# Strassen's scheme in the last FFN stage of two token tiles, and DMA transposes for the local heads of the last batch

## The chip, the cores and the metric

The kernel runs on one core of one Trainium2 chip. The metric is the device time of one execution in microseconds. Four executions of the kernel before took 269.8, 269.98, 270.36 and 271.9 us, with a median of 270.17 us.

## What is computed

The reference is sparse attention followed by a multiplicative feed-forward network (FFN):

```python
batch, n_heads, seq, head_dim = (8, 8, 576, 64)
mask_local = (rel >= 0) & (rel < 32)                                  # heads 0 to 3
mask_strided = (rel >= 0) & (pos[None, :] % 32 == pos[:, None] % 32)  # heads 4 to 7
attn = softmax(where(mask, scale * q @ k.T, -1e9)) @ v
x = attn.transpose(0, 2, 1, 3).reshape(4608, 512)
out = ((x @ w1) * (x @ w2)) @ w3 @ w_out        # w1, w2: 512 x 1024, w3: 1024 x 1024, w_out: 1024 x 512
```

Inputs and output are float32. The kernel multiplies in float16 and adds up in float32.

## The kernel before

**Planner.** The kernel is a list of operations (`plan.op`) with an engine, an assumed duration, dependencies, buffer slots taken and given back, and a rank. `Plan.order` plays this list through once with its own assumed durations and so fixes one order for each engine; the operations are then emitted in that order. Semaphores come from the dependencies of the tiles, in program order. SP issues all DMAs, in one queue.

**Stages.** The product w34 = w3 @ w_out is formed first. Attention goes batch by batch, and within a batch by pairs of heads: pairs 0 and 1 are local, 2 and 3 strided. For each pair there are scores on TensorE (`ps_S`, L795), the Exp on ACT (L812), the mask on DVE (L819) and the product with v (`ps_X`, L831 or L843). A strided pair is normalised by Ln and Exp on ACT and a product on DVE, straight into `xT` (L904). A local pair is normalised on DVE into `xqs` (L866, L867) with the token on the partition; six TensorE transposes (`ps_U`, L924) and one DVE copy then bring it into `xT`. A second way exists in the code: from batch `UB` on, the local pair is normalised into `xqd` and a DMA transpose on SP (L914) writes `xT`. `UB` is 8 before, so it is not used. `xT[0]` to `xT[3]` hold the attention output, feature on the partition and token on the free axis, one tile for each pair of heads.

**FFN.** There are nine tiles of 512 tokens. For tiles 0 to 6, each of eight columns jc of 128 features has four matmuls with w1 (`ps_a`, L1119), four with w2 (`ps_b`, L1135), an ACT copy of a, and a DVE product into `abt` (L1141). Then each of four blocks of 128 tokens has eight matmuls of 128x512 with w34 (`ps_o`, L1155), an ACT copy into `osb` (L310) and a store.

**The last two tiles**, tA = 7 and tB = 8, use Strassen's scheme (in Winograd's form) for the columns named in `sf`, which before are 1 to 7. The two tiles and the two halves of the 512 input features make a 2x2 block matrix, w1 and w2 with the same halves the other one. Seven products P1 to P7 of two matmuls each (L1053) replace eight. The sums of inputs are called S1 to S4 (L990, on POOL and DVE), the differences of weights T1 to T4 (L965, POOL). The products are gathered in a bank A (`ps_Aw`) and in a tile of two banks, E and G (`ps_Bw`), in this order: P1 into A, P5 into G, A copied onto E by ACT (`e`), P6 into A, G copied out by ACT (`p5`), P2 into E, A copied out (`u2`), P7 into A, G plus u2 on DVE (`u4`, L1076), E copied out (`c11`), A plus p5 on DVE (`c22`, L1084), P3 into G, P4 into A, and at last the two products into `abt` (L1088, L1091). Column 0 is done in the plain way for both tiles, and all eight output blocks of the two tiles are plain. The last block is split by columns into 256, 128 and 128.

Of the kernel before, what the change touches and what calls it, by code (L numbers as in the profile page):

```python
# [24 lines left out]
def _loads():  # L25
# [6 lines left out]
    for b in range(2, 8):  # L32
# [6 lines left out]

CFG = dict(loads=_loads(), arank=_arank, frank=lambda j: 50 + j, slack=100,  # L40
           pord=lambda b: (2, 3, 0, 1) if b < 2 else (0, 1, 2, 3), tsplit=False, dmaf=1.08, nhr=8, cast=dict(w1=dict(POOL=1040)),
           first=('DVE', 'ACT', 'POOL'), early=0, pm=4, nx=4, nstg=8, new=(2, 3), lb=3, ll=4, nat={'POOL': 1160}, sf=(1, 2, 3, 4, 5, 6, 7), te={'POOL': 2150}, nr=(1, 25, 2, 0), te1='POOL', se=((3, 0), (3, 1), (1, 0), (2, 0), (4, 0)))


def _ap(t: bass.AP, off_add, dims):
# [215 lines left out]
def kernel(  # L261
# [38 lines left out]
    NABT = cfg.get("nabt", 3)  # L300
    stgs = [consts.tile([P, DF], FP32, name=f"st{i}") for i in range(NSTG)]
    plan = Plan(dict(f=NF, B=2, stg=NSTG, asb=2, osb=3, rcp=2, xqs=2, xqd=cfg.get("nxq", 2), w3n=3, abt=NABT,
                     u2=2, p5=2, c11=2, c22=2))

    def pin(ins):
        return tc.keep_in_program_order(ins)
# [259 lines left out]
    def load_qs(b, hp):  # L566
        hh, local = hp % 2, hp < 2
        b1 = LL if local else LB
        for nm, ten in (("q", q), ("k", k)):
            key = f"{nm}s{b}_{hp}"  # L570
            if local:
                ds = [dma(key, key, 880, [P, 2, LT, D], lambda s: s[0:LQ].rearrange("p h c d -> p h (c d)"),
                          ten[b, 2 * hp:2 * hp + 2].rearrange("h (p c) d -> p h (c d)", c=LT))]
            else:
                ds = load_s(key, ten, b, hp)
            nr, nt = (LQ, LT) if local else (SC, ST)

            def fn(e, nm=nm, key=key, nr=nr, nt=nt):
                t = qkp.tile([nr, nt, 2, D], FP16, tag=f"{nm}{hp // 2}", name="xs16")
                copy(e, t.rearrange("p c h d -> p h c d"), stg[key][0:nr])  # L580
                x16[(b, nm, hp)] = t

            c = cast("c" + key, key, ds, {"POOL": 825} if local else POOL, fn)
            late.append((c, lambda nm=nm: [DTop[(b - 1, nm, hp)]] if b > b1 else
                         [Top.get((b - 2 + hh, h)) for h in (hp - hh, hp - hh + 1)]))

            def ft(e, nm=nm, key=key, nr=nr, nt=nt):
                if local:
                    o = live[key] = ffn.tile([P, nt * nr], FP16, tag="w3n", bufs=3, name="qk8")
                elif nm == "q":  # L590
                    o = qT[:, hp]
                else:
                    o = kTS[:, hh, 0:ST * SC]
                pin(nc.sync.dma_start(o.rearrange("x (c w) -> x c w", w=nr),
                                      x16[(b, nm, hp)].rearrange("p c h d -> p (c h d)"), transpose=True))
# [352 lines left out]
    smul, sfirst = {}, []  # L948
    if SF:
        W = {(1, 1): w1h[:, 0:2], (1, 2): w2h[:, 0:2], (2, 1): w1h[:, 2:4], (2, 2): w2h[:, 2:4]}  # L950
        T, Tt = {}, {}
# [47 lines left out]
        if cfg.get("te1", "POOL") == "POOL":  # L999
            gate = plan.op("gate", {"POOL": 200}, lambda e: pin(  # L1000
                nc.gpsimd.tensor_copy(out=scr, in_=St[1][:, 1, 1, 0:2])), deps=[Sx[(4, 1)], T[(4, 0)]], rank=11)
            for i in range(1, 5):
                T[(i, 1)].deps.append(gate)
        SL = lambda j: (lambda c: St[j // 3][:, (j - 1) % 2 if j < 3 else j - 3, c])
        A = {1: lambda c: xT[c][:, tk1], 2: lambda c: xT[2 + c][:, tk1], 4: lambda c: xT[2 + c][:, tk2]}
        sd = lambda i: [Sx[(i, 0)], Sx[(i, 1)]]
# [8 lines left out]
    for n_, jc in enumerate(SF):  # L1015
# [75 lines left out]
            nc.vector.tensor_mul(big[("abt", tB)][:, jc, :], bk("A"), tmp["c22"])), [q4], give=[kA, tk["c22"]])  # L1091
        smul[(tA, jc)], smul[(tB, jc)] = h1, h2

    def frk(t, jc):
        if not SF or t < tA:
            return 100 + 24 * t + 2 * jc + 1
        i = [x for x in range(KF) if x not in SF].index(jc)
        return 100 + 24 * tA + cfg.get("nr", (1, 25, 2, 0))[t - tA] + cfg.get("nr", (1, 25, 2, 0))[2] * i

    for t in range(NTILE):  # L1100
# [9 lines left out]
        for jc in range(KF):  # L1110
            js = bass.ds(jc * P, P)
            if (t, jc) in smul:
                muls.append(smul[(t, jc)])
                continue

            def fa(e, jc=jc, t=t, js=js, tok=tok):
                ps = bank("f", f"a{t}_{jc}", [P, NT], FP32)
                for ci in range(KM):
                    pin(nc.tensor.matmul(ps, w1h[:, ci, js], xT[ci][:, tok], start=(ci == 0), stop=(ci == KM - 1)))  # L1119

            a = plan.op(f"a{t}_{jc}", {"PE": 864}, fa, deps=[z] + w1c[jc] + (xd if t in zs else []), take=[("f", f"a{t}_{jc}")],
                        rank=frk(t, jc))

            def fs(e, jc=jc, t=t):
                asb = ffn.tile([P, NT], FP32, tag="asb", bufs=2, name="asb")
                live[("asb", t, jc)] = asb
                copy(e, asb, bank("f", f"a{t}_{jc}"))

            s = plan.op(f"asb{t}_{jc}", cfg.get("asb", {"ACT": 590}), fs, deps=[a], take=[("asb", f"{t}_{jc}")],
                        give=[("f", f"a{t}_{jc}")], rank=4)  # L1130

            def fb(e, jc=jc, t=t, js=js, tok=tok):
                ps = bank("f", f"b{t}_{jc}", [P, NT], FP32)
                for ci in range(KM):
                    pin(nc.tensor.matmul(ps, w2h[:, ci, js], xT[ci][:, tok], start=(ci == 0), stop=(ci == KM - 1)))  # L1135
# [7 lines left out]
            muls.append(plan.op(f"mul{t}_{jc}", {"DVE": 690}, fu, deps=[bb, s],  # L1143
                                give=[("f", f"b{t}_{jc}"), ("asb", f"{t}_{jc}")], rank=4))
        for ts in range(NT // P):
# [76 lines left out]
```

## Time and profile before

| | value |
|---|---|
| median of the four runs | 270.17 us |
| profiled execution | 270.19 us, of which the span of the trace is 268.2 us |
| granted TensorE clock, mean | 0.998 |
| first `ps_U` of batch 7, second `ps_U` | 205.12 us, 210.68 us |
| last `ps_X` of batch 7 | 219.98 us |
| first plain column of tile 7 | 224.57 us |
| first P5 | 228.02 us |
| last output matmuls issued from | 252.86 us on, without a break |
| first copy of the last block | 263.94 us |

The page gives the busy time of each engine in the span. Matmuls are pipelined: a row of the timeline that says 0.43 us may have its successor start after 0.27 us, and the distance of the starts is what the path pays. Windows give the same busy times stretch by stretch. The chain of waits goes back from the last instruction to what released each one.

### The profile page before, as it was taken

The page shows a single profiled execution, that of the slowest core. Times are in us where ns is not written, and L with a number is a line of the kernel's source. Part 1 is how long each engine was busy: PE and PEld are TensorE (multiplying, and loading weights), DVE is VectorE, ACT ScalarE, POOL GpSimd, SP SyncE. Part 2 cuts the span into 40 slices and gives each one's busy share as a digit, 9 for nine tenths or more (in the row PEclk, how much of TensorE's full clock was granted, in tenths as well). Part 3 has the DMA queues.
Part 4 walks back from the last instruction along what each step waited for, and adds up shares of the span by engine and source line. Part 5 has one row for each costly group of instructions (what it writes and reads, how often), then busy time and mean ns, then how long its engine had stood idle before and what let it go on. Part 6 is the DMA issues. An engine that isn't in the chain of part 4 may idle for free.

```text
span 268.2 us, 6079 instructions
## 1 busy us (share of the span) xinstructions
PE 256.2 (96%) x2251; PEld 140.0 (52%) x2251; DVE 179.1 (67%) x342; ACT 162.3 (61%) x293; POOL 169.2 (63%) x186
## 2 busy tenths in 40 slices
PE   6787799999999999999999999999999999999994
PEld 2466687545655555554554454455445554434443
DVE  6744566885787748866875788479748865678601
ACT  2780467774666785577477557764785576577241
POOL 6676897769979716955795479617999553900000
PEclk9999999999999999999999999999999999999999
DMA  7999999999799988899999998999994004000053
GB/s 248 316 367 287 302 355 353 323 247 283 282 287 212 175 214 224 192 175 288 225 180 183 280 251 171 194 281 205 179 211 149 2 0 156 0 2 0 0 197 121
DMA packets 72766, 54.41 MB, mean 203 GB/s; under 512 B 44256, under 2 KB 62048, under 8 KB 72736
## 3 DMA queue, kind: packets, MB, share of 16 engines
q1 hardware_dynamic: 72736, 54.02, 82.7%
q8 instruction: 18, 0.29, 0.5%
q14 instruction: 12, 0.10, 0.1%
HBM read 38.93 MB, written 9.44 MB: 180 GB/s over the span
## 4 chain that ended last, share of the span: by engine, by line
PE 86%; DMA 8%; POOL 1%; DVE 1%; ACT 1%; SPq 1%; issue 1%; POOLq 0%; DVEq 0%
PE ps_o L1155 23%; PE ps_b L1135 19%; PE ps_a L1119 18%; DMA st<-in_moe_w_dram 6%; PE ps_Aw L1053 4%; PE ps_S L795 4%; PE ps_Bw L1053 3%; PE ps_mm L670 3%; PE ps_X L843 3%; PE ps_X L831 3%; PE ps_U L924 2%; DMA st<-in_q_dram 2%; PE ps_T L748 2%; SPq L317 1%; POOL w3n L314 1%
## 5 line engine op out<-in xcount | busy, mean ns | idle before, releaser
L1155 PE MATMUL ps_o<-w,abt 128*128 128x512 f16 (+2 forms) x304 | 67.9, 368 | 0.0
L1135 PE MATMUL ps_b<-xT,w2h 128*128 128x512 f16 x232 | 59.4, 379 | 0.2 <-DVE kTL L312 0.2
L1119 PE MATMUL ps_a<-xT,w1h 128*128 128x512 f16 x232 | 59.6, 379 | 0.0
L310 ACT COPY asb<-ps_a 128x512 f32<-128x512 f32 x58 | 34.0, 589 | 31.0 <-PE ps_a L1119 29.9
L1141 DVE TENSOR_TENSOR abt<-ps_b,asb 128x512 f16<-128x512 f32 x58 | 39.9, 688 | 7.6 <-PE ps_b L1135 6.4
L314 POOL CAST xs<-st 80x1024 f16<-80x1024 f32 (+1 forms) x36 | 33.3, 941 | 17.0 <-DMA st<-in_k_dram 10.1
L812 ACT ACTIVATE ps_S<-ps_S 128x576 f32<-128x576 f32 (+2 forms) x56 | 32.9, 627 | 16.3 <-PE ps_S L795 16.3
L1155 PEld LDWEIGHTS <-abt 128*128 128x128 f16 x304 | 27.6, 98 | 28.2 <-issue 0.2
L904 DVE TENSOR_TENSOR xT<-ps_X,rcp 64x288 f16<-64x288 f32 x56 | 25.2, 450 | 18.3 <-ACT rcp L888 17.8
L1135 PEld LDWEIGHTS <-w2h 128*128 128x128 f16 x232 | 21.6, 98 | 23.7 <-issue 0.7
L310 ACT COPY osb<-ps_o 128x512 f32<-128x512 f32 (+1 forms) x36 | 20.3, 581 | 17.8 <-PE ps_o L1155 17.6
L314 POOL CAST v16L<-st 32x768 f16<-32x768 f32 (+1 forms) x32 | 26.3, 823 | 7.0 <-DMA st<-in_v_dram 5.5
L1119 PEld LDWEIGHTS <-w1h 128*128 128x128 f16 x232 | 20.2, 99 | 18.5
L819 DVE TENSOR_TENSOR ptm<-ps_S,maskL 128x576 f16<-128x576 f32 x28 | 19.9, 753 | 9.1 <-ACT ps_S L812 8.9
L867 DVE TENSOR_TENSOR xqs<-ps_X,rcq 96x384 f16<-96x384 f32 (+1 forms) x36 | 20.5, 568 | 1.2
L314 POOL CAST v16S<-st 72x1024 f16<-72x1024 f32 (+1 forms) x16 | 16.5, 1037 | 7.2 <-DMA st<-in_v_dram 7.2
L877 ACT ACTIVATE ps_X<-ps_X 64x576 f32<-64x576 f32 x28 | 17.7, 631 | 3.8 <-PE ps_X L831 3.2
L888 ACT ACTIVATE rcp<-ps_X 64x576 f32<-64x576 f32 x28 | 18.2, 648 | 0.9
L843 PEld LDWEIGHTS <-ptm 128*96 128x96 f16 (+1 forms) x224 | 14.6, 123 | 5.8 <-issue 0.2
L670 PE MATMUL ps_mm<-woh,xT 128*128 128x256 f16 x128 | 16.0, 273 | 1.4 <-POOL woh L314 1.4
L314 POOL CAST x<-st 128x1024 f16<-128x1024 f32 x14 | 14.4, 1038 | 3.6 <-DMA st<-in_q_dram 1.7
L819 DVE TENSOR_TENSOR ptm<-ps_S,maskK 72x576 f16<-72x576 f32 x20 | 14.1, 746 | 2.5 <-ACT ps_S L812 2.5
(113 smaller groups left out, 358.4 us busy)
## 6 DMA issues: line engine op xcount, KB each, us to landing
out_dram<-osb SPq DMA_DIRECT2D x35, 256.0 KB
st<-in_moe_w_dram SPq DMA_DIRECT2D x16, 512.0 KB
st<-in_v_dram SPq DMA_DIRECT2D x16, 288.0 KB
st<-in_v_dram SPq DMA_DIRECT2D x16, 256.0 KB
st<-in_q_dram SPq DMA_DIRECT2D x7, 512.0 KB
st<-in_k_dram SPq DMA_DIRECT2D x7, 512.0 KB
st<-in_q_dram SPq DMA_DIRECT2D x10, 256.0 KB
st<-in_k_dram SPq DMA_DIRECT2D x10, 256.0 KB
```

The source lines that it names most:

```text
L310: pin(nc.scalar.copy(out=out, in_=in_))
L314: pin(nc.gpsimd.tensor_copy(out=out, in_=in_))
L670: pin(nc.tensor.matmul(ps, w3T(kc)[:, js], big["woh"][:, kc, ns], start=(kc == 0), stop=(kc == KF - 1)))
L812: pin(nc.scalar.activation(out=sps, in_=sps, func=AF.Exp, bias=0.0, scale=scale))
L819: pin(nc.vector.tensor_mul(ptm[0:kr, 0:576].rearrange("p (h a x) -> p h a x", h=2, x=w), pte[0:kr].rearrange("p h (a x) -> p h a x", x=w), ...
L843: pin(nc.tensor.matmul(xps[0:w, h, i * 65:(i + 1) * 65], ptms[pslot][0:kr, c0:c0 + w], vt[0:kr, 2 * (hp % 2) + h, g * m + i, 0:D + 1], sta ...
L867: pin(nc.vector.tensor_mul(xqs[0:w, 0:m].rearrange("p i h d -> p h i d"), xv[:, :, :, 0:D], _ap(rcp, 0, [[rcp.ap[0][0], w], [4, 2], [1, m] ...
L904: pin(nc.vector.tensor_mul(o, i0, i1))
L1119: pin(nc.tensor.matmul(ps, w1h[:, ci, js], xT[ci][:, tok], start=(ci == 0), stop=(ci == KM - 1)))
L1135: pin(nc.tensor.matmul(ps, w2h[:, ci, js], xT[ci][:, tok], start=(ci == 0), stop=(ci == KM - 1)))
L1141: pin(nc.vector.tensor_mul(big[("abt", t)][:, jc, :], bank("f", f"b{t}_{jc}"), live[("asb", t, jc)]))
L1155: pin(nc.tensor.matmul(ps, big[("abt", t)][:, ci, bass.ds(ts * P, P)], w34[:, ci, bass.ds(n0, nw)], start=(ci == 0), stop=(ci == KF - 1)))
```

## The change

Four things are changed.

- **Output by Strassen.** For the token blocks 0 and 1 (`so=(0, 1)`) of both last tiles, the product with w34 is done by the same scheme. The blocks are: a token block of tile 7 over one of tile 8, the halves of the 1024 features of `abt` (jc 0 to 3, jc 4 to 7), and w34 cut in two by features and in two by its 512 output columns. One product is four matmuls of 128x256. The differences of w34 go to POOL (`O1` to `O4`), the sums of `abt` to DVE except the third, which goes to POOL (`Z`). The results are put together in float32 in parts of `xT` that are no longer read (`o7`, `o8`) and stored from there. Blocks 2 and 3 stay plain.
- **Which columns are plain.** `sf` is now 0 to 6, so column 7 is plain in the two last tiles.
- **Local heads of batch 7** (`ub=7`) go through `xqd` and two DMA transposes; `nxq=3` gives `xqd` three buffers.
- A key of `x16` is renamed, with no effect.

The planner orders everything anew with this list; the order of the instructions before tile 6 is the same as before.

```diff
-           ... sf=(1, 2, 3, 4, 5, 6, 7), te={'POOL': 2150}, ...)
+           ... sf=(0, 1, 2, 3, 4, 5, 6), te={'POOL': 2150}, ..., so=(0, 1), ro=42, ub=7, nxq=3)
...
+    def out_strassen():
+        HN = DM // 2
+        hh = {(1, 1): (tA, 0), (1, 2): (tA, 4), (2, 1): (tB, 0), (2, 2): (tB, 4)}
+        W = {(i, j): w34[:, 4 * i - 4:4 * i, bass.ds(HN * (j - 1), HN)] for i in (1, 2) for j in (1, 2)}
...
+            T[i] = plan.op(f"O{i}", {"POOL": 2150}, ftt, deps=w34op + [T1last, T.get(1), T.get(2)],
+                           take=[("stg", f"O{i}")] if i in (1, 2) else [], rank=14, lock=True)
...
+        for n_, ts in enumerate(SO):
+            Sx = {}
+            for i in (3, 1, 2, 4):
...
+                d = {3: md(tA, 1) + md(tB, 1), 1: md(tB, 1) + md(tB, 2), 2: md(tA, 1), 4: md(tA, 2)}[i]
+                Sx[i] = plan.op(f"Z{i}_{ts}", {"POOL": 1150} if i == 3 else {"DVE": 430}, fss,
+                                deps=d + ([Sx[i // 2]] if i in (2, 4) else []), rank=3.9 + .01 * n_, lock=True)
+            kA, kB = ("f", f"Ao{ts}"), ("B", f"Bo{ts}")
+            prods = dict(P1=(lambda ts=ts: ah(1, 1, ts), lambda: W[(1, 1)], "A", md(tA, 1) + w34op),
+                         P5=(lambda ts=ts: sv(1, ts), lambda: Tt[1], "G", [Sx[1], T[1]]),
+                         P6=(lambda ts=ts: sv(2, ts), lambda: Tt[2], "A", [Sx[2], T[2]]),
+                         P2=(lambda ts=ts: ah(1, 2, ts), lambda: W[(2, 1)], "E", md(tA, 2)),
+                         P7=(lambda ts=ts: sv(3, ts), lambda: Tt[3], "A", [Sx[3], T[3]]),
+                         P4=(lambda ts=ts: ah(2, 2, ts), lambda: Tt[4], "A", md(tB, 2) + [T[4]]),
+                         P3=(lambda ts=ts: sv(4, ts), lambda: W[(2, 2)], "G", [Sx[4]]))
...
+                    for c in range(4):
+                        pin(nc.tensor.matmul(bk(x), lf()[:, c], rt()[:, c], start=st_ and c == 0, stop=c == 3,
+                                             skip_group_check=not st_))
...
+            ce_ = vec("e", AC, lambda e, bk=bk: copy(e, bk("E"), bk("A")), [q1, q5])
+            q6 = prod("P6", extra=[ce_], rank=.5)
+            c5 = vec("p5", AC, lambda e, bk=bk, new=new: copy(e, new("p5"), bk("G")), [q5], take=["p5"])
+            q2 = prod("P2", extra=[ce_], rank=.6)
+            cu = vec("u2", AC, lambda e, bk=bk, new=new: copy(e, new("u2"), bk("A")), [q6], take=["u2"])
+            q7 = prod("P7", extra=[cu], rank=1)
+            g = vec("u4", DV, lambda e, bk=bk, tmp=tmp: pin(nc.vector.tensor_add(bk("G"), bk("G"), tmp["u2"])),
+                    [cu, c5], give=[tk["u2"]])
+            c22 = vec("c22", DV, ..., [q7, c5], take=["o8"], give=[tk["p5"]])
+            c11 = vec("c11", AD, lambda e, bk=bk, new=new: copy(e, new("o7")[:, 0:HN], bk("E")), [q2], take=["o7"])
+            q3 = prod("P3", extra=[g], rank=1.1)
+            q4 = prod("P4", extra=[c22], rank=1.2)
+            c12 = vec("c12", AD, lambda e, bk=bk, tmp=tmp: copy(e, tmp["o7"][:, HN:DM], bk("G")), [q3, c11], give=[kB])
+            c21 = vec("c21", AD, lambda e, bk=bk, tmp=tmp: copy(e, tmp["o8"][:, 0:HN], bk("A")), [q4, c22], give=[kA])
...
         for ts in range(NT // P):
+            if t in zs and ts in SO:
+                continue
```

In the new order, the TensorE stream from the end of tile 6 is: P1 of columns 0, 1 and 2, P5 of 0 and 1, P6 and P2 of 0, the plain a of tile 7 column 7, and so on through the seven columns; the plain output halves of tile 7 (blocks 2 and 3) stand among the last Strassen products of the FFN. The output products then come in this order (the last digit is the token block): P1-0, P4 of column 6, second halves of blocks 2 and 3 of tile 7, P5-0, P1-1, first half of block 2 of tile 8, P6-0, P2-0, P5-1, P7-0, P3-0, P6-1, P4-0, P2-1, P7-1, P3-1, second half of block 2, P4-1, and the split block 3. On SP, the two DMA transposes stand after the last stores of tile 5 and ahead of those of tile 6.

More of the change, by code (lines that the diff above doesn't have):

```diff
@@ L41 @@
            pord=lambda b: (2, 3, 0, 1) if b < 2 else (0, 1, 2, 3), tsplit=False, dmaf=1.08, nhr=8, cast=dict(w1=dict(POOL=1040)),
-           first=('DVE', 'ACT', 'POOL'), early=0, pm=4, nx=4, nstg=8, new=(2, 3), lb=3, ll=4, nat={'POOL': 1160}, sf=(1, 2, 3, 4, 5, 6, 7), te={'POOL': 2150}, nr=(1, 25, 2, 0), te1='POOL', se=((3, 0), (3, 1), (1, 0), (2, 0), (4, 0)))
+           first=('DVE', 'ACT', 'POOL'), early=0, pm=4, nx=4, nstg=8, new=(2, 3), lb=3, ll=4, nat={'POOL': 1160}, sf=(0, 1, 2, 3, 4, 5, 6), te={'POOL': 2150}, nr=(1, 25, 2, 0), te1='POOL', se=((3, 0), (3, 1), (1, 0), (2, 0), (4, 0)), so=(0, 1), ro=42, ub=7, nxq=3)
 def _ap(t: bass.AP, off_add, dims):
@@ L302 @@
     plan = Plan(dict(f=NF, B=2, stg=NSTG, asb=2, osb=3, rcp=2, xqs=2, xqd=cfg.get("nxq", 2), w3n=3, abt=NABT,
-                     u2=2, p5=2, c11=2, c22=2))
+                     u2=2, p5=2, c11=2, c22=2, ob=4))
     def pin(ins):
@@ L580, in fn @@
                 copy(e, t.rearrange("p c h d -> p h c d"), stg[key][0:nr])
-                x16[(b, nm, hp)] = t
+                x16[(b, nm, "s", hp)] = t
             c = cast("c" + key, key, ds, {"POOL": 825} if local else POOL, fn)
@@ L594, in ft @@
                 pin(nc.sync.dma_start(o.rearrange("x (c w) -> x c w", w=nr),
-                                      x16[(b, nm, hp)].rearrange("p c h d -> p (c h d)"), transpose=True))
+                                      x16[(b, nm, "s", hp)].rearrange("p c h d -> p (c h d)"), transpose=True))
             o = DTop[(b, nm, hp)] = plan.op(f"D{nm}{b}_{hp}", {"SP": 1300}, ft, deps=[c], dma=cfg.get("dtc", (1080, 1200))[0 if local else 1], store=True,
@@ L947 @@
     tk1, tk2 = bass.ds(tA * NT, NT), bass.ds(tB * NT, NT)
-    smul, sfirst = {}, []
+    smul, sfirst, mul = {}, [], {}
     if SF:
@@ L1003 @@
                 T[(i, 1)].deps.append(gate)
+        T1last = T[(4, 1)]
         SL = lambda j: (lambda c: St[j // 3][:, (j - 1) % 2 if j < 3 else j - 3, c])
@@ L1092, with ftt, ah, sv @@
         smul[(tA, jc)], smul[(tB, jc)] = h1, h2
+    SO = cfg.get("so", ()) if SF else ()
+    def out_strassen():
+        HN = DM // 2
+        hh = {(1, 1): (tA, 0), (1, 2): (tA, 4), (2, 1): (tB, 0), (2, 2): (tB, 4)}
+        W = {(i, j): w34[:, 4 * i - 4:4 * i, bass.ds(HN * (j - 1), HN)] for i in (1, 2) for j in (1, 2)}
+        T, Tt = {}, {}
+        for i, x, y in ((1, (1, 2), (1, 1)), (3, (2, 2), (1, 2)), (2, (2, 2), 1), (4, (2, 1), 2)):
+            def ftt(e, i=i, x=x, y=y):
+                if i in (1, 2):
+                    raw = stgs[plan.slot[("stg", f"O{i}")]].bitcast(FP16).rearrange("p (i k n) -> p i k n", i=2, k=4)
+                    Tt[i], Tt[{1: 3, 2: 4}[i]] = raw[:, 0], raw[:, 1]
+                b0 = Tt[y] if isinstance(y, int) else W[y]
+                eng = nc.gpsimd if e == "POOL" else nc.vector
+                pin(eng.tensor_sub(Tt[i], W[x], b0))
+            T[i] = plan.op(f"O{i}", {"POOL": 2150}, ftt, deps=w34op + [T1last, T.get(1), T.get(2)],
+                           take=[("stg", f"O{i}")] if i in (1, 2) else [], rank=14, lock=True)
+        def ah(i, j, ts):
+            t, c0 = hh[(i, j)]
+            return big[("abt", t)][:, c0:c0 + 4, bass.ds(ts * P, P)]
+        def sv(i, ts):
+            return xT[i - 1][:, 0:4 * NT].rearrange("p (k n) -> p k n", k=4)[:, :, bass.ds(ts * P, P)]
+        md = lambda t, k: [mul[(t, jc)] for jc in range(4 * k - 4, 4 * k)]
+        for n_, ts in enumerate(SO):
+            Sx = {}
+            for i in (3, 1, 2, 4):
+                def fss(e, i=i, ts=ts):
+                    eng = nc.gpsimd if e == "POOL" else nc.vector
+                    f = eng.tensor_add if i == 1 else eng.tensor_sub
+                    a0 = {3: lambda: ah(1, 1, ts), 1: lambda: ah(2, 1, ts), 2: lambda: sv(1, ts), 4: lambda: ah(1, 2, ts)}
+                    a1 = {3: lambda: ah(2, 1, ts), 1: lambda: ah(2, 2, ts), 2: lambda: ah(1, 1, ts), 4: lambda: sv(2, ts)}
+                    pin(f(sv(i, ts), a0[i](), a1[i]()))
+                d = {3: md(tA, 1) + md(tB, 1), 1: md(tB, 1) + md(tB, 2), 2: md(tA, 1), 4: md(tA, 2)}[i]
[9 more added lines that the diff above has]
+                         P3=(lambda ts=ts: sv(4, ts), lambda: W[(2, 2)], "G", [Sx[4]]))
+            tmp = {}
+            def bk(x, kA=kA, kB=kB):
+                return (bank(*kA) if x == "A" else bank(*kB)[:, "EG".index(x)])[:, 0:HN]
+            def new(nm, tmp=tmp, ts=ts):
+                if nm[0] == "o":
+                    tmp[nm] = xT[plan.slot[("ob", f"{nm}o{ts}")]][:, 4 * NT:6 * NT].bitcast(FP32)
+                else:
+                    tmp[nm] = qkp.tile([P, HN], FP32, tag=TAG[nm], bufs=2, name=nm)
+                return tmp[nm]
+            def prod(nm, extra=(), take=(), rank=0, ts=ts, kA=kA, kB=kB, prods=prods, bk=bk):
+                lf, rt, x, d = prods[nm]
+                def fn(e):
+                    if nm == "P1":
+                        bank(*kA, [P, NT], FP32)
+                    if nm == "P5":
+                        live[kB] = seen[plan.slot[kB]]
+                    st_ = nm in ("P1", "P5")
+                    for c in range(4):
+                        pin(nc.tensor.matmul(bk(x), lf()[:, c], rt()[:, c], start=st_ and c == 0, stop=c == 3,
+                                             skip_group_check=not st_))
+                return plan.op(f"{nm}o{ts}", {"PE": 440}, fn, deps=d + list(extra), take=take,
+                               rank=100 + 24 * tA + cfg.get('ro', 30) + 3 * n_ + rank, soft=True)
+            def vec(nm, eng, fn, deps, give=(), take=()):
+                return plan.op(f"{nm}o{ts}", eng, fn, deps=deps, give=list(give),
+                               take=[("ob" if x[0] == "o" else x, f"{x}o{ts}") for x in take], rank=3 + .1 * n_)
+            AC, DV, AD = {"ACT": 370}, {"DVE": 400}, {"ACT": 370, "DVE": 380}
+            tk = {x: ("ob" if x[0] == "o" else x, f"{x}o{ts}") for x in ("u2", "p5", "o7", "o8")}
+            q1 = prod("P1", take=[kA], extra=sfirst)
+            q5 = prod("P5", take=[kB], extra=[q1], rank=.1)
+            ce_ = vec("e", AC, lambda e, bk=bk: copy(e, bk("E"), bk("A")), [q1, q5])
[6 more added lines that the diff above has]
+                    [cu, c5], give=[tk["u2"]])
+            c22 = vec("c22", DV, lambda e, bk=bk, new=new, tmp=tmp: pin(
+                nc.vector.tensor_add(new("o8")[:, HN:DM], bk("A"), tmp["p5"])), [q7, c5], take=["o8"], give=[tk["p5"]])
+            c11 = vec("c11", AD, lambda e, bk=bk, new=new: copy(e, new("o7")[:, 0:HN], bk("E")), [q2], take=["o7"])
[3 more added lines that the diff above has]
+            c21 = vec("c21", AD, lambda e, bk=bk, tmp=tmp: copy(e, tmp["o8"][:, 0:HN], bk("A")), [q4, c22], give=[kA])
+            for t, o, c in ((tA, "o7", c12), (tB, "o8", c21)):
+                plan.op(f"st{o}_{ts}", {"SP": 450}, lambda e, o=o, t=t, ts=ts, tmp=tmp: pin(
+                    nc.sync.dma_start(out_r[t * (NT // P) + ts], tmp[o])), deps=[c], give=[tk[o]], rank=4.5, dma=750,
+                        store=True)
@@ L1144 @@
                                 give=[("f", f"b{t}_{jc}"), ("asb", f"{t}_{jc}")], rank=4))
+        if t in zs:
+            mul.update({(t, jc): m for jc, m in enumerate(muls)})
+        if SO and t == tB:
+            out_strassen()
         for ts in range(NT // P):
+            if t in zs and ts in SO:
+                continue
             last = t == NTILE - 1 and ts == NT // P - 1
```

## The prediction

> **What bounds the kernel now.** I read the busy shares of the page first, then the windows, then the PE timeline and the chain of waits of the last 45 us.
>
> ```profile
> PE 256.2 (96%) x2251; PEld 140.0 (52%) x2251; DVE 179.1 (67%) x342; ACT 162.3 (61%) x293; POOL 169.2 (63%) x186
> ...
> PE 86%; DMA 8%; POOL 1%; DVE 1%; ACT 1%; SPq 1%; issue 1%; POOLq 0%; DVEq 0%
> ```
>
> ```profile
> 200.00:210.00 10.00, 10.00 (x81) 5.28 (x80) 8.32 (x17) 5.22 (x10) 10.00 (x6) 1.00 0.47 129
> 210.00:220.00 10.00, 10.00 (x101) 5.12 (x100) 7.94 (x14) 6.89 (x13) 3.83 (x5) 1.00 0.01 2
> ...
> 240.00:250.00 10.00, 10.00 (x47) 4.48 (x46) 8.06 (x13) 6.43 (x12) 0.00 (x0) 1.00 0.00 0
> 250.00:260.00 10.00, 10.00 (x48) 4.52 (x47) 3.18 (x5) 3.13 (x6) 0.00 (x0) 1.00 0.29 106
> ```
>
> The columns of a window are its length and the busy us of PE, PEld, DVE, ACT and POOL, then granted clock, DMA share and GB/s. TensorE is full in all of them at clock 1.00: from about 40 us to 264 us it sets the time, so a microsecond of TensorE work removed, or of a TensorE wait added, is a microsecond of span. DMA is empty from 208 us and POOL from 234 us. The last stages do have waits, which the chain shows:
>
> ```profile
> 234.41 0.58 ACT ps_Bw L310
> 234.99 0.04 issue
> 235.03 0.59 PE ps_Aw L1053 x2
> 235.62 0.03 issue
> 235.65 0.61 PE ps_Bw L1053 x2
> 236.25 0.02 issue
> 236.27 0.60 ACT c L310
> 236.87 0.02 issue
> 236.89 0.71 DVE ps_Bw L1076
> 237.60 0.04 issue
> 237.65 0.59 PE ps_Bw L1053 x2
> ```
>
> In one Strassen group a product waits for a copy or an addition of the partial sum before. Links: PE to ACT about 0.2 us after the last matmul's issue slot (235.65 plus two slots of 0.216 is 236.08; ACT starts at 236.27), ACT to DVE 0.02 us, DVE to PE 0.05 us. The DVE addition here starts only after ACT's copy of the other half of the same PSUM tile: operations on one tile follow each other in program order even where they touch different halves.
>
> **Part 1, local heads of batch 7 by DMA.** Twelve TensorE transposes (ps_U) and two DVE copies go (0.46 us each, covered); two DMA transposes come. The price of the transposes:
>
> ```profile
> 205.12 0.43 PE L924 MATMUL ps_U<-id,xqs 96*128 96x96 f16 x6
> 205.39 1.03 PE L1135 MATMUL ps_b<-xT,w2h 128*128 128x512 f16 x4
> ```
>
> The next row starts 0.27 us later, and so at 210.68 to 210.95: two times 0.27 is **-0.53 us** on the path. The DMAs stand on SP behind three stores of tile 5 and ahead of the stores of tile 6. They are issued when the second norm of each head pair is done (about 204.2 and 210.3), take 1.23 us of SP each (the 36 existing transposes have that median), and delay no store, as tile 6's first output copy ends near 220.6. Their landing has no direct row; an existing one, issued at 192.49 amid loads, released POOL at 197.69, so at most 5.2 us. Below, one cannot beat its issue of 1.23 us. I take 4 (the queue is nearly empty), that is 208 and 214. First reader is POOL's difference S3, free until S1_0 can start at about 217.8 (third head pair); TensorE reads the two tiles at about 223.8. Even 5.2 us costs nothing; without cover, the landing would have to pass 222 before TensorE waits.
>
> **Part 2, the output stage.** Four blocks of 8 matmuls 128x512 become 14 products of 4 matmuls 128x256. Old: 32 x 0.216 = 6.91 us (four matmuls are 0.86 in the chain). New: the nearest row is the w3 stage:
>
> ```profile
> 32.27 1.92 PE L670 MATMUL ps_mm<-woh,xT 128*128 128x256 f16 x16
> 34.02 0.65 PE L785 MATMUL ps_S<-biasL,id 128*128 128x288 f16 x4
> ```
>
> 1.75 us for 16 is 0.110 each; 56 x 0.110 = 6.16: **-0.75 us**. A rule speaks against this: the Trainium skill, "TensorE: Matmul & The Clock Gate", section "The mechanism", has a weight load overlap matmuls in flight only where the row group differs. All loads here fill all rows, at 98 ns. Unhidden, 56 x (0.110 + 0.098) = 11.6 us would replace 32 x (0.216 + 0.098) = 10.0, a loss of 1.6. The row decides: 16 full-row loads and matmuls fit in 1.75, so loads are hidden at 256 columns too. Bounds of the term: -0.79 (0.1094 each) to -0.7.
>
> Helpers: POOL gets four weight differences of 2.09 us from 234.9 (they queue behind the old T ones) and two S3 sums of about 1.2, ending at 245.7; their first readers on TensorE come at 253.3 (O1) and 256.4 (S3 sums). DVE gets six sums of 0.42 after its last abt product. The first: last P4 ends 251.6, +0.2, product 0.69, sum 0.42, links 0.1, is 253.0; two plain output halves (1.73 us) stand before P5, which can start at 253.35. Hidden by 0.3.
>
> What isn't hidden is the accumulation chain, now on products of 0.44 us. Durations for 256 columns:
>
> ```profile
> L310 ACT CAST w<-ps_mm 128x256 f16<-128x256 f32 x4 | 1.5, 373 | 3.9 <-PE ps_mm L670 3.9
> ...
> L312 DVE CAST w<-ps_mm 128x256 f16<-128x256 f32 x12 | 5.1, 424 | 6.0 <-PE ps_mm L670 5.7
> ```
>
> By tile order u4 (DVE, adds into the second half) waits for P2, c11 (copies the first half) for u4, and P3 for c11. Block 0: 0.2 + 0.43 + 0.02 + 0.37 + 0.05 = 1.07 us after P2; between P2 and P3 stand P5 of block 1 and P7 (0.88): wait 0.2. Block 1: c11 is on DVE, 0.2 + 0.43 + 0.05 + 0.43 + 0.05 = 1.16; only P7 (0.44) stands between: wait 0.72. Sum **+0.92 us**. No row shows these two waits. Below, 0.3, if the halves of a tile are not held apart (P3 after u4 only: block 1's 0.73 less 0.44); above 1.6, if u2, c22 and the second e copy, whose margins are 0.2 to 0.3, slip by one copy in each block. The chain above is the nearest row, with the same order, so I take 0.92. So the Strassen output alone is slightly a loss, -0.75 + 0.92.
>
> **Part 3, what moves.** The plain FFN column goes from 0 to 7 and later in the order; the matmul count is the same. Before, 224.57 to 252.86 is 28.29 us for 126 matmuls (27.2): 1.1 us of waits, read singly 0.15, 0.39, 0.19, 0.28, 0.07, 0.06. In the new order the 0.39 (P6 after a copy with one P1 between) and the 0.28 (P3) keep their neighbours. The 0.19 goes: a P4 now stands between P6 and P2. The 0.15 goes, as the plain column stands later. New is the head: three plain groups (2.6 us) no longer stand between tile 6 and Strassen, so the first P5 meets the last DVE sum S1_1. From the last ps_X: Ln and Exp behind the pair before, 0.65 each, two norms 0.91, sum 0.42; this ends at about 225.4, where P5's second matmul would issue at 225.28: wait 0.15. New waits 0.15 + 0.39 + 0.28 + 0.1 = 0.9: **-0.2 us**. Bounds: 0 to -0.5. The strided scores of the last heads move one output half later (S7_3 to 218.5); in tile 6 every gap is filled by plain matmuls, 0.
>
> **Tail.** The last block is split as before, the same three copies and three small stores follow. One 256 KB store more is issued in the last 2 us; at the 16 engines' 350 GB/s seen in the loading stage that is 0.75 us, with DMA at 0.37 share there: 0, above 0.3.
>
> Sum: -0.53 - 0.75 + 0.92 - 0.2 = -0.56; I take **-0.6** (the small waits of block 0 read slightly high against the same kind in the chain). The profiled execution took 270.19 us, span 268.2 and 2.0 around it; its median of four is 270.17. So span 267.6, time **269.6**.
>
> **Rivals.**
> - *Waits are filled* (0.12): P3 waits only for u4 and the head's wait vanishes. -0.53 - 0.77 + 0.3 - 0.5 = -1.5: 268.7. For it: halves lie in different banks. Against: the chain above.
> - *Output waits eat everything* (0.17): 1.6 instead of 0.92 gives 0.1 gained: 270.1. For it: margins of 0.2 to 0.3 us on ACT and DVE, where one late copy passes to the next. Against: the stage before ran with like margins and lost 1.1 in 28 us.
> - *The head goes late* (0.09, slower): the last heads' chain from S7_3 to S1_1 is 6.9 us and starts now 6.5 us before P5 instead of 10.4. Every further microsecond on it (an osb copy of 0.59 ahead of the Exp, a mask behind an abt product) is one of TensorE. From 0.6 us more than counted the kernel is slower; three such copies, 1.8, give 271.4. Against: ACT and DVE have idle time there in the windows (6.9 and 7.9 of 10).
> - *DMA transposes land late* (0.02): needs over 10 us against 5.2: 272.
>
> The forecast's own case has 0.6. From no change 0.5%, 1.35 us, is about what a measurement here can tell. Faster than 268.8: most of the first rival and a little of the forecast, 0.13. Slower than 271.5: half of the last two, 0.06. Within: 0.81. Range: 268.7 to 270.6, from the first rival's end to the second with a run's scatter.
>
> **What would show it.** No ps_U rows after 200 us; the first Strassen product near 223.8; a wait on the first P5 of 0.1 to 0.3; two waits before P3 on the xT operand between 256 and 261, about 0.2 and 0.7, released by ACT and DVE copies; the last matmul issued about 0.6 us earlier; no wait on DMA. A span under 267 with no such waits, or a wait over 0.8 on the first P5, would prove me wrong.

## The result and the profile after

The changed kernel takes 269.49 us (median of 44 runs, 268.57 to 270.95); the kernel before took 270.23 us in 63 runs beside it (269.38 to 271.9). The ratio is 0.9969, 95% interval 0.9959 to 0.9979: 0.8 us less. The forecast was 269.6 us. The profiled execution took 269.65 us, with a span of 267.9 us, against 270.19 and 268.2 before.

The first view is again the page of the changed kernel: the busy shares and the head of the chain.

```profile
PE 255.8 (96%) x2263; PEld 142.2 (53%) x2263; DVE 184.1 (69%) x354; ACT 162.0 (60%) x297; POOL 179.6 (67%) x192
...
PE 13%; DVE 1%; ACT 1%; issue 0%; DVEq 0%
```

Sums of busy time show nearly nothing: PE is 0.4 us less in a span 0.3 us shorter. The 13% do not mean that TensorE stopped being the bound. The chain is followed back here only to 225.42 us, just before a DVE sum for which the profile knows no releaser, and the rest of the span is missing from the shares. The windows are the same view as before the change; their columns are length, busy us of PE, PEld, DVE, ACT and POOL, clock, DMA share, GB/s.

```profile
200.00:210.00 10.00, 10.00 (x78) 5.20 (x77) 7.68 (x16) 5.39 (x10) 9.92 (x7) 1.00 0.88 184
210.00:220.00 10.00, 10.00 (x89) 4.84 (x88) 6.30 (x11) 6.04 (x12) 5.14 (x5) 1.00 0.09 16
...
250.00:260.00 10.00, 9.64 (x68) 6.51 (x67) 6.02 (x15) 3.95 (x10) 0.00 (x0) 1.00 0.20 74
```

From 200 us on, TensorE is as full as before (from 230 to 240 us it was busy for 9.63 of 10 us and now is for 9.66), except in the output stage. There it has many more and shorter matmuls and, for the first time, holes. The chain of waits of the changed kernel names two of them:

```profile
255.99 0.45 PE ps_Bw L1167 x4
...
256.53 0.44 DVE ps_Bw L1187
...
257.00 0.38 ACT xT L310
...
257.42 0.60 PE ps_Bw L1167 x4
258.02 0.87 PE ps_Ao L1167 x8
258.89 0.45 PE ps_Bw L1167 x4
...
259.43 0.44 DVE ps_Bw L1187
...
259.90 0.43 DVE xT L312
...
260.38 0.60 PE ps_Bw L1167 x4
```

Line 1187 is `u4`, the addition into the second half of the tile. The rows at 257.00 (on ACT) and 259.90 (on DVE) are `c11`, the copy of its first half, and those at 257.42 and 260.38 are P3 of the two blocks. P3 adds into the second half alone and uses nothing that `c11` makes, and still it starts 0.04 to 0.05 us after that copy. In the PE timeline the waits are:

```profile
256.70 0.60 PE L1167 MATMUL ps_Ao<-st,xT 128*128 128x256 f16 x4
257.42 0.60 PE L1167 MATMUL ps_Bw<-w,xT 128*128 128x256 f16 x4
...
259.16 0.60 PE L1167 MATMUL ps_Ao<-st,xT 128*128 128x256 f16 x4
260.38 0.60 PE L1167 MATMUL ps_Bw<-w,xT 128*128 128x256 f16 x4 [0.61 <-DVE xT L312]
```

The starts are 0.72 and 1.22 us apart, where a product takes 0.44: waits of 0.28 and 0.78 us.

**Stages of TensorE.** Three marks cut the end of the kernel: the first matmul of tile 6, the first FFN matmul of the last two tiles, and the start of the first copy out of the split last block. That copy starts 0.2 us after the last matmul of its own part; in every kernel three or four short matmuls of the other two parts still run behind it. The rest, up to the end of the span, is the tail; as the span is given to 0.1 us, the tail is good to 0.05 us. The rows are from the timeline of one execution each, in us; the experiments are told below.

| | tile 6 begins | tile 6 | last FFN and output | tail |
|---|---|---|---|---|
| before | 199.82 | 24.75 | 39.37 | 4.26 |
| after | 199.97 | 24.29 | 39.37 | 4.27 |
| e1_no_dmat | 199.44 | 24.74 | 39.73 | 4.19 |
| e2_no_out | 199.89 | 24.23 | 39.17 | 4.31 |
| e3_known | 200.99 | 24.24 | 38.32 | 5.05 |
| e4_before_dmat | 200.11 | 24.24 | 39.17 | 4.48 |
| e7_ffn | 201.04 | 24.24 | 38.20 | 4.92 |
| e12_out1 | 200.37 | 24.24 | 38.72 | 3.97 |
| e13_ub6 | 200.45 | 24.23 | 39.38 | 3.84 |
| e14_act | 200.48 | 24.24 | 38.32 | 5.06 |
| e15_before_act | 200.60 | 24.74 | 39.37 | 4.99 |
| e17_halves | 199.57 | 24.24 | 38.31 | 4.68 |
| e18_known2 | 200.32 | 24.23 | 38.32 | 5.03 |

The two middle columns repeat to about 0.02 us for like kernels (one value, the 24.29, stands 0.05 apart), so differences of 0.1 us can be read in them. The tail does not repeat so well: it is 4.26, 4.31 and 4.48 us in three kernels with the plain output on SP (before, e2_no_out, e4_before_dmat), and 4.27 and 3.84 in two with the same output stage (after, e13_ub6). Nor does the time of a whole run: tile 6 begins anywhere from 199.4 to 201.0 us. That spread is there before the first FFN matmul, which comes at 43.8 to 45.4 us; from it to tile 6 every kernel but e13_ub6 takes 155.62 or 155.63 us. The table says at once where the gain lies. Tile 6 is 0.46 us shorter, and the stage that was rewritten takes as long as before.

### The profile page after: what moved, and what is told of

Same layout as the page of the kernel before. It is cut to its first block, busy times and chain, and to the rows that moved or that the text cites. A ratio compares the mean times of both kernels' runs of the same rounds, so it can differ in the third digit from the quotient of the medians.

```text
span 267.9 us, 6128 instructions
## 1 busy us (share of the span) xinstructions
PE 255.8 (96%) x2263; PEld 142.2 (53%) x2263; DVE 184.1 (69%) x354; ACT 162.0 (60%) x297; POOL 179.6 (67%) x192
## 5 line engine op out<-in xcount | busy, mean ns | idle before, releaser
L1268 PE MATMUL ps_o<-w,abt 128*128 128x512 f16 (+2 forms) x272 | 61.3, 367 | 0.0
L904 DVE TENSOR_TENSOR xT<-ps_X,rcp 64x288 f16<-64x288 f32 x56 | 25.2, 450 | 18.2 <-ACT rcp L888 17.7
L1268 PEld LDWEIGHTS <-abt 128*128 128x128 f16 x272 | 24.4, 98 | 23.7
L310 ACT COPY osb<-ps_o 128x512 f32<-128x512 f32 (+1 forms) x32 | 18.0, 580 | 16.6 <-PE ps_o L1268 15.1
L867 DVE TENSOR_TENSOR xqs<-ps_X,rcq 96x384 f16<-96x384 f32 (+1 forms) x32 | 18.2, 570 | 1.1
```

The lines of the kernel that those rows point to most:

```text
L310: pin(nc.scalar.copy(out=out, in_=in_))
L867: pin(nc.vector.tensor_mul(xqs[0:w, 0:m].rearrange("p i h d -> p h i d"), xv[:, :, :, 0:D], _ap(rcp, 0, [[rcp.ap[0][0], w], [4, 2], [1, m] ...
L904: pin(nc.vector.tensor_mul(o, i0, i1))
L1268: pin(nc.tensor.matmul(ps, big[("abt", t)][:, ci, bass.ds(ts * P, P)], w34[:, ci, bass.ds(n0, nw)], start=(ci == 0), stop=(ci == KF - 1)))
```

## The experiments

**Theory A** (the prediction's): the DMA transposes bring their TensorE time, Strassen in the output stage gives back all that it saves in two waits on the order within one tile, and the moved plain column brings 0.2 us. **Rivals:** the output product itself is dearer than its matmuls (weight loads that aren't hidden, helpers on DVE and ACT); or the DMA transposes bring nothing and something else in the new order does.

**Without the DMA transposes**, and **without Strassen in the output stage**, each from the changed kernel:

```diff
# e1_no_dmat
-so=(0, 1), ro=42, ub=7, nxq=3
+so=(0, 1), ro=42, nxq=3
# e2_no_out
-so=(0, 1), ro=42, ub=7, nxq=3
+ub=7, nxq=3
```

> The changed kernel with the local heads of batch 7 turned on TensorE again. Theory: the output by Strassen alone is -0.75 of matmuls and +1.0 of waits before P3, and the order of the FFN stage falls back to that of the kernel before with its 1.1 us of waits; so about 0.3 us slower than before, 270.5. Rival A (the output by Strassen carries the gain, the DMA transposes nothing): 269.5, as the changed kernel. Rival B (both carry their matmul counts in full, the waits are slack): 269.5 too, with no waits of 0.2 and 0.7 before P3.

> The changed kernel without the output by Strassen: DMA transposes and columns 0 to 6 stay. Theory: it keeps -0.53 of ps_U and -0.2 to -0.4 of FFN waits, 269.3, that is 0.2 us faster than the changed kernel. Rival A (the output carries the gain): 270.2. Rival B: 269.9 to 270.0.

Measured: e1_no_dmat 270.15 us, ratio 0.9998 [0.9980, 1.0015]; e2_no_out 269.37 us, 0.9968 [0.9954, 0.9982]. Without the DMA transposes none of the gain is left, and leaving Strassen out of the output changes nothing that the runs can tell. In the stages, the output by Strassen costs 0.20 us (39.37 against 39.17).

**The kernel before, with only the DMA transposes added:**

```diff
# e4_before_dmat, from the kernel before
-se=(... (4, 0))
+se=(... (4, 0)), ub=7, nxq=3
```

> The kernel before with the DMA transposes for batch 7 alone, columns 1 to 7. Theory: the choice of the plain column moves nothing by itself, the new order of the FFN stage comes with the transposes; 269.3, as the changed kernel without the output by Strassen. Rival D (column 0 instead of 7 in Strassen brings the shorter waits of the FFN stage): 269.7.

Measured: 268.86 us, 0.9957 [0.9942, 0.9972], at least as good as the whole change. This kernel has the plain column at 0 and e2_no_out has it at 7, with nothing else between them; tile 6 and the last stage agree to 0.01 us. So the choice of the plain column is worth nothing, and the 0.2 us that the prediction gave it must be somewhere else. The PE timeline shows where. First e1_no_dmat (plain column 7, no DMA transposes), then e4_before_dmat (plain column 0, with them), from the first FFN matmul of the last two tiles on:

```profile
224.18 1.03 PE L1226 MATMUL ps_a<-xT,w1h 128*128 128x512 f16 x4
225.04 1.03 PE L1242 MATMUL ps_b<-xT,w2h 128*128 128x512 f16 x4
225.90 1.03 PE L1226 MATMUL ps_a<-xT,w1h 128*128 128x512 f16 x4
226.77 1.03 PE L1054 MATMUL ps_Aw<-xT,w1h 128*128 128x512 f16 x4
```

```profile
224.35 1.47 PE L1053 MATMUL ps_Aw<-xT,w1h 128*128 128x512 f16 x6
225.66 1.23 PE L1053 MATMUL ps_Bw<-st,st 128*128 128x512 f16 x4
226.72 0.59 PE L1053 MATMUL ps_Aw<-st,st 128*128 128x512 f16 x2
227.18 0.59 PE L1053 MATMUL ps_Bw<-xT,w1h 128*128 128x512 f16 x2
```

With the six-transpose groups gone, the planner begins with Strassen products and puts the plain groups later, whichever column is plain; with them, it puts three plain groups first, as before. Why its rules choose so was not followed up. The waits follow: e1_no_dmat has those of the kernel before (0.15, 0.39, 0.19, 0.28 and twice 0.06 us, 1.13 in all; one of 0.16 more comes between the first output product and P4 of column 6), e4_before_dmat those of the changed one (0.20, 0.39, 0.28; 0.87). The 0.2 us of the FFN stage belongs to the DMA transposes (`ub=7` with its `nxq=3`).

**The planner told of the waits.** P3 waits for `c11` and `c11` for `u4`, although neither needs the other's result; what they share is the tile. The planner's list of dependencies doesn't say so. Adding this changes no work, only the order:

```diff
# e3_known, from the changed kernel, in out_strassen
-            c11 = vec("c11", ..., [q2], take=["o7"])
-            q3 = prod("P3", extra=[g], rank=1.1)
+            c11 = vec("c11", ..., [q2, g], take=["o7"])
+            q3 = prod("P3", extra=[g, c11], rank=1.1)
```

> The changed kernel with two dependencies more in the plan only: c11 after u4, and P3 of the output after c11. These exist on the chip anyway through the shared PSUM tile; now the planner knows them and may put other output matmuls into the waits. Theory: both waits before P3 (0.28 and 0.78) are filled and 1.0 us goes, 268.5. Rival C (the waits stand for full ACT and DVE queues, so they only move to the next product): 269.3 to 269.5.

Measured: 268.6 us (7 runs), 0.9941 [0.9923, 0.9959]; the same kernel came to 0.9967 in a second set of runs (e18_known2, below), so the runs don't show that it is faster than the changed one. The stages do. Both waits are gone. In the PE timeline of e3_known, P3 of block 1 now stands late, behind the split block's first matmuls:

```profile
260.72 0.60 PE L1268 MATMUL ps_o<-w,abt 128*128 128x256 f16 x4
261.16 0.60 PE L1167 MATMUL ps_Ao<-st,xT 128*128 128x256 f16 x4
261.59 0.61 PE L1268 MATMUL ps_o<-w,abt 128*128 128x128 f16 x8
262.04 0.60 PE L1167 MATMUL ps_Bw<-w,xT 128*128 128x256 f16 x4
262.48 0.60 PE L1167 MATMUL ps_Ao<-st,abt 128*128 128x256 f16 x4
```

Starts are 0.44 us apart for four 128x256 or eight 128x128 matmuls, that is 0.109 and 0.056 us each, with no hole. The stage is 38.32 us: 1.05 us shorter than that of the changed kernel, where the two waits were 1.06. This excludes the rival that the product is dear in itself: without waits, Strassen on two blocks is 0.85 us faster than the plain output (39.17). That the shared tile is the reason for the order was not tested by itself, as no kernel gave the two halves tiles of their own. And the tail grew from 4.27 to 5.05 us.

**The same told to the planner in the FFN stage:**

```diff
# e7_ffn, from e3_known, in the FFN's Strassen after c11, for all but the first columns
+            g.deps.append(c11)
```

> The kernel with the two added dependencies, and the same one for the FFN products: u4 after c11 in the plan (from the third column on). The wait of 0.28 before a P3 of the FFN stage is in the kernel before too, by the same chain. Theory: it is filled, two small ones of 0.1 appear elsewhere: 0.2 us less than with the output's dependencies alone, ratio to the kernel before 0.993. Rival C (waits only move): no difference, 0.994, with another wait of 0.3.

Measured: 268.97 us, 0.9958 [0.9942, 0.9975]: a miss. Of the three waits the one of 0.28 us went, 0.21 and 0.39 stayed, and one of 0.08 came. The stage gained 0.12 us, which is too little for the runs to show.

**Only one of the two output blocks by Strassen:**

```diff
# e12_out1, from e3_known
-so=(0, 1)
+so=(0,)
```

> The kernel with the two added dependencies, Strassen for token block 0 only, block 1 plain. Theory: without waits a block is worth its matmuls, 0.4 us, so the kernel lies half way between the one without the output by Strassen (0.9968) and the one with both blocks (0.9941): 0.9955. Rival (what was gained by the added dependencies is another order, not the blocks): 0.994.

Measured: 269.78 us, 0.9990 [0.9959, 1.0021]: one of the twelve runs took 918 us, and the others scattered too much to say anything. The stage says more: 39.17 us with no block, 38.72 with one, 38.32 with two. Each block by Strassen, without waits, is worth 0.40 to 0.45 us; half of the 0.78 us less of matmuls would be 0.39.

**DMA transposes for batch 6 too:**

```diff
# e13_ub6, from the changed kernel
-ub=7
+ub=6
```

> The changed kernel with DMA transposes for the local heads of batch 6 too, while inputs are still being loaded. Theory: 12 more TensorE transposes go, -0.5, but the queue of SP is not free there and the landing is later than 2.7 us; what TensorE or POOL wait is at most the 5.2 us seen amid loads less its cover: between -0.5 and +1.0, most likely +0.5, with a wait of TensorE between 195 and 210 us. Rival E (DMA transposes are free wherever they stand): -0.5, ratio 0.995.

Measured: 269.96 us, 0.9993 [0.9969, 1.0018], as the likeliest value expected. By the medians the gain of batch 7 is lost again, though the interval just reaches the 0.9969 of the changed kernel. The trace says it more clearly: from the first matmul of tile 5 to that of tile 6 this kernel takes 25.79 us, where the others take 25.20. Its PE timeline shows a hole ahead of tile 6 that the changed kernel doesn't have:

```profile
199.00 0.30 PE L795 MATMUL ps_S<-qT,kTL 64*128 64x96 f16 x6
200.21 0.30 PE L795 MATMUL ps_S<-qT,kTL 64*128 64x96 f16 x6 [0.91 <-DVE xT L904]
200.45 1.04 PE L1226 MATMUL ps_a<-xT,w1h 128*128 128x512 f16 x4
```

Batch 6's transposes meet a full queue: between 191 and 201 us SP issues four other DMA transposes and nine loads or stores, and the two new ones, at 180.1 and 190.1 us, hold SP for 4.12 and 1.21 us. That the late loads make the wait was not tried by itself; shown is a new wait of 0.91 us, which ends with a DVE product of another pair of heads (L904) and uses up the gain. In batch 7 SP issues nothing but the two transposes between 204.8 and 221.1 us.

**The tail.** e3_known won 1.05 us on TensorE, and lost 0.78 us behind its last copy. The SP queues of the changed kernel and of e3_known, in this order:

```profile
262.48 0.85 SPq L1289 DMA_DIRECT2D out_dram<-osb  x1
263.43 0.38 SPq L1198 DMA_DIRECT2D out_dram<-xT  x1
264.08 1.32 SPq L1289 DMA_DIRECT2D out_dram<-osb  x3
```

```profile
263.20 1.46 SPq L1198 DMA_DIRECT2D out_dram<-xT  x2
264.75 1.64 SPq L1289 DMA_DIRECT2D out_dram<-osb  x3
```

In e3_known the last 256 KB store, behind another issued 0.4 us earlier, holds SP for 1.03 of the 1.46 us, where the median issue of these stores is 0.39. The three small stores begin 1.20 us after the last block's first copy starts, against 0.45 in the changed kernel. **Theory T1**: SP's issue is late. **T2**: the data itself takes that long. Two kernels moved the small stores to ACT's queue, from e3_known and from the kernel before:

```diff
# e14_act and e15_before_act
-plan.op(f"st{key}", cfg.get("st", {"SP": 450}), fd, deps=[c],
+plan.op(f"st{key}", {"ACT": 450} if last else cfg.get("st", {"SP": 450}), fd, deps=[c],
```

> The kernel with the two added dependencies in the output stage; the three small stores of the split last block are issued by ACT instead of SP. In the profile without this, TensorE's last copy came 1.05 us earlier in its stage than in the changed kernel, but the tail behind it was 0.78 longer: SP's issue of the 256 KB store before took 1.03 us instead of 0.33 and held the first small store from 263.97 to 264.75. Theory: SP's queue backs up behind two large stores close together; from ACT the small stores start at once, the tail falls from 5.05 to about 4.3, ratio 0.991 to 0.992. Rival F (the DMA engines themselves are full, 256 KB twice at 350 GB/s): the small stores land no earlier, ratio 0.994.

> Control: the kernel before with the same three small stores on ACT. There the large store before them is issued 1.2 us earlier and takes 0.33. Theory: no gain, ratio 0.999 to 1.001. Rival F: no gain either. A gain of over 0.3 us would mean that issuing on ACT is faster by itself, and that the other run doesn't speak for a backed up queue.

Measured: e14_act 269.66 us, 0.9944 [0.9914, 0.9974] (before 270.71 beside it); e15_before_act 271.04 us, 1.0008 [0.9987, 1.0028]. In e14_act the stores do leave early:

```profile
262.69 1.46 SPq L1198 DMA_DIRECT2D out_dram<-xT  x2
263.26 0.27 ACT L310 COPY osb<-ps_o 128x128 f32<-128x128 f32 x1 [1.94 <-PE ps_o L1268]
263.49 1.49 ACTq L1289 DMA_DIRECT2D out_dram<-osb  x3
```

They begin 0.45 us after the first copy starts, 0.75 us sooner than in e3_known, but the last packet comes 3.5 us after that copy against 3.7, and the tail is 5.06 us all the same. The runs of the control show no change, as expected. But in its trace the tail is 4.99 us against 4.26, although the small stores leave as early as in the kernel before:

```profile
265.16 2.12 ACTq L1176 DMA_DIRECT2D out_dram<-osb  x3
```

The first copy starts at 264.71, so that is 0.45 us in both. But the first of the three issues takes 1.14 us on ACT, where on SP it took 0.41, and the last packet comes 3.4 us after the copy and not 2.7. In e14_act that first issue took 0.37 us, so the two kernels lose their time in different places, and this pair can't judge T1.

The last pair stayed on SP, and sent half of each of block 1's two results before the other half was ready:

```diff
# e17_halves, from e3_known; e18_known2 is e3_known again
+parts = ((c0, x, HN), (c, HN - x, HN)) if n_ == len(SO) - 1 else ((c, 0, DM),)
+for k_, (d_, n0, nw) in enumerate(parts):
-    nc.sync.dma_start(out_r[t * (NT // P) + ts], tmp[o])
+    nc.sync.dma_start(out_r[t * (NT // P) + ts][:, n0:n0 + nw], tmp[o][:, n0:n0 + nw])
```

> The output stage with the waits filled (as e3_known), and the stores of the last x tiles of block 1 issued in halves, so that less data stands in front of the small stores at the very end. If the 0.7 to 0.8 us that e3_known lost behind its last copy was the issue of small stores behind a large store still under way, TensorE's stage stays at 38.3 us, the tail comes down from 5.0 to 4.3-4.5 us, and the kernel is 0.4 to 0.7 us faster than e3_known on the same chip (ratio to before about 0.992). If the end is held by all of the outgoing data or by the end of the program, the tail stays at about 5.0 us and the ratio at 0.994.

> The kernel of e3_known again, to stand beside e17_halves on one chip: ratio to before 0.994 as in its first run, TensorE's last stage 38.3 us, tail about 5.0 us. If the tail of the first run was an accident of that execution, it is 4.3 us here and the ratio 0.991.

Measured on one chip: e17_halves 269.04 us, 0.9949 [0.9925, 0.9973]; e18_known2 269.55 us, 0.9967 [0.9943, 0.9991]. The long tail is no accident (5.03 us again). With halved stores it is 0.35 us shorter, a little under what was expected, and the ratio of about 0.992 that was expected was not reached. As tails of like kernels differ by up to 0.43 us in the table, one trace doesn't prove the 0.35. Nor is it as T1 has it:

```profile
261.77 1.48 SPq L1200 DMA_DIRECT2D out_dram<-xT  x2
263.34 1.36 SPq L1291 DMA_DIRECT2D out_dram<-osb  x3
```

The small stores leave 1.22 us after the first copy's start, as late as in e3_known; only less data is outstanding, and the traffic ends about 3.4 us after that copy instead of 3.7. How much of the tail is issue and how much data stays open.

On the long issue itself the traces hold a hint. Beside the stores they have a second kind of traffic, here in e3_known from 258 us on (packets, MB, share of the 16 engines):

```profile
q8 instruction: 1, 0.02, 0.5%
```

It is one read of 16 KB, named "instruction", from 263.33 to 264.27 us. In all six kernels in which an issue of a store near the end takes 0.85 us or more on SP (the changed one, e3_known, e7_ffn, e14_act, e17_halves, e18_known2), such a read is under way when that issue begins, and the issue ends 0.37 to 0.39 us after it, about the length of an ordinary issue. In the others no issue on SP near the end takes over 0.42 us; e1_no_dmat has one of 0.33 us that falls within such a read, so the overlap alone isn't enough. It looks as if SP waits there for its own next instructions, but no kernel moved the read to test it.

e17_halves has the smallest sum of stages and tail of the kernels with both blocks by Strassen, 67.23 us against 67.93 of the changed kernel and 68.38 before. Its ratio of 0.9949 and the 0.9957 of e4_before_dmat, the two-option change, can't be told apart.

## Why the prediction was right, point by point

- **Local heads by DMA, −0.53.** Measured −0.46 in the changed kernel, and −0.50 to −0.52 against the kernel before in the other kernels that have it. No `ps_U` rows come after 200 us. The two DMAs are issued at 205.01 and 210.47 and hold SP for 1.23 and 1.20 us. POOL starts the sum that reads the second tile at 213.15, so it landed within 2.7 us, not 4; the profile shows no wait of TensorE for a DMA after 200 us.
- **Output matmuls, −0.75.** Four take 0.435 to 0.44 us: 56 x 0.1095 = 6.13 us for 6.91, which is −0.78. A full-row weight load of 98 ns stays hidden under a matmul of 109. The rule that the prediction cites from the Trainium skill ("TensorE: Matmul & The Clock Gate", "The mechanism"), by which a load overlaps only where the row group differs, would by the prediction's estimate have made this stage 1.6 us longer; the 38.32 us of e3_known, 0.85 less than the plain 39.17, exclude that. The same section also lets a load into a background weight buffer be pulled ahead, which the prediction leaves out; no run here shows whether that is what hides the loads. Of the 0.85 us, 0.07 are not in this term and stay unexplained.
- **Waits before P3, +0.92.** 0.28 + 0.78 = 1.06 us. The order of the operations is the one named, and e3_known shows what it costs by filling the waits. The size was low by 0.14, mostly in one term, the link from the last matmul of P2 to DVE: taken as 0.2 us behind its issue slot, it is 0.27 in block 0 (P2 starts at 255.82 and has 0.44, DVE starts at 256.53) and 0.26 in block 1.
- **FFN stage, −0.2.** The size was right by luck and the cause wrong. The step read "the plain column goes from 0 to 7 and later in the order" and "the 0.15 goes, as the plain column stands later". e1_no_dmat has the plain column at 7 and still stands with three plain groups first and 1.13 us of waits; e4_before_dmat has it at 0 and stands with the new head. The head moves with `ub=7`, which takes work out of the planner's list. As a result the DMA transposes are worth 0.7 us, not 0.53, and the rest of the change costs 0.25 in the stages, not the 0.03 of gain (−0.75 + 0.92 − 0.2) that the sum gave it. The wait on the first P5, foreseen as 0.15, is 0.2 and stands beside its cause in the chain of the changed kernel:

```profile
225.51 0.43 DVE st L990
225.94 0.04 issue
225.99 0.81 PE ps_Bw L1054 x3
```

(The table of the profile before puts the last `ps_X` of batch 7 at 219.98 us. In that trace the last group starts at 220.85; at 219.98 stands the output half behind the group before it. The prediction's chain starts from the scores and does not use the figure.)

- **Tail, 0.** 4.27 against 4.26 us; that it agrees to 0.01 is chance, as e13_ub6 has 3.84 with the same end.
- **Sum, −0.56.** The stages and the tail give −0.45, the profiled executions −0.54, the runs −0.84 with an interval of −0.57 to −1.11. The range, 268.7 to 270.6, was wide enough to hold no change at all. What supports the prediction is that its terms were found one by one, and of these one, the FFN stage, was right for a wrong reason and the tail by chance. Against the sum of stages and tail, the runs of e4_before_dmat are 0.7 us better and those of e12_out1 1.2 us worse. With a start of tile 6 that scatters over 1.6 us, one trace each can't settle that; it stays open.
- **The rivals.** "Waits are filled" was false of this kernel: P3 waited for `c11` and not only for `u4`. Its lower bound of 0.3 us should have been 0.24 (0.2 + 0.43 + 0.05 − 0.44; the prediction has 0.73 for the first three). When the planner is told (e3_known), the two holes do vanish, but by another order. "Output waits eat everything" came close: the output stage alone did give back all that it saved and 0.2 us more, but the rest of the gain stood. Its own sum had a wrong sign: 1.6 for 0.92 turns −0.56 into +0.12, a loss, so about 270.3 and not 270.1. "The head goes late" would have shown a wait over 0.6 on P5, which is 0.2. "DMA transposes land late" needed over 10 us; the second landed within 2.7.

## What to carry to other kernels

Where a scheduler sets the order, an option that removes work moves other work as well: change one option at a time before a gain is put down to one of them. Fewer multiplications pay only as far as the partial sums are ready: tell the scheduler of every wait that the tiles bring, two halves of one tile included, since an unfilled microsecond costs what a saved one brings (here 1.06 us of waits stood against 0.78 us of matmuls). At the end of the kernel, a stage that ends sooner also bunches its stores: count what is still outstanding behind the last copy.

## What the runs showed that was not expected

The issue of a store on SP is not of one length: the store of the results takes 0.33 to 0.38 us in most cases of the last stage, and 0.85 to 1.05 for some near the end, each of these beside a read of instructions. A DMA transpose held SP for 1.2 us with nothing else issued beside it and once, amid loads, for 4.12. Issuing three small stores from a second engine's queue made the tail longer by 0.7 us (4.26 to 4.99) though they left no later. A DMA transpose of 96x768 values landed within 2.7 us with nothing else issued beside it, where one amid loads had taken up to 5.2. And most of the scatter of the profiled executions arises before the first FFN matmul, 1.6 us of it; from there to tile 6 the kernels with one order agree to 0.01 us.
